# Clustered attention and a gated MLP on one core: the attention loop in four stages of three units a pair instead of six periods of two

## The chip, the cores and the metric

The kernel runs on one core of one Trainium2 chip. The metric is the device time of one execution in microseconds (us), the median of three runs. A core has a matrix engine (TensorE, PE in the profile; its weight loads are shown apart as PEld), a vector engine (VectorE, DVE), a scalar engine for functions of one input (ScalarE, ACT), a general engine (GpSimd, POOL) and SyncE (SP), which here issues transfers. Each engine works through its own queue in order; they wait for one another by semaphores. Operands lie in SBUF (128 partitions); matmuls write to PSUM, which has eight banks of 512 fp32 numbers in each partition.

## What is computed

Two blocks, one after the other, all in float32:

```python
# attention: q, k, v of (4, 8, 768, 64); 16 centroids a head
q_assign = argmax(einsum('bhsd,hcd->bhsc', q_n, c_n), axis=-1)   # q_n, k_n, c_n: normalized
k_assign = argmax(einsum('bhsd,hcd->bhsc', k_n, c_n), axis=-1)
mask = q_assign[:, :, :, None] == k_assign[:, :, None, :]
scores = where(mask, q @ k^T / sqrt(64), -1e9)
attn = exp(scores - max(scores)); attn = attn / (sum(attn) + 1e-9)
out = attn @ v
# bridge to x of (3072, 512), then the MLP, w_in (512, 2048), w_out (2048, 512)
h = x @ w_in
g = h * erf(softplus(h))
return g @ w_out
```

A query sees only the keys of its own cluster.

## The kernel before

**Pairs, halves, units.** The 32 heads are taken two at a time: 16 pairs (`p`), the two heads (`e`) in the two halves of the partitions. A pair has two halves of 384 queries, and for each half six tiles of 128 keys: 12 units (`u`), 192 in all. The order of every engine's work is that of the program text: the wrapper `InOrder` (lines 50 to 64) keeps it, and line 59 is therefore the line of nearly every row of the profile. One tells rows apart by their tiles.

**What a unit needs.** `products(u)` (line 405) writes the fp32 products of keys and queries to a PSUM tile `sc`, of which there are two (line 109). `scores(u)` (line 418) adds to the same tile a bf16 product of the masks `km` and `qm`, which brings a large negative number where clusters differ and subtracts a bound on the maximum. `curve(u)` (line 431) is ScalarE's exponential from `sc` to one of eight SBUF tiles `pr`; an `sc` tile is free for the unit after next once its curve has read it. `accumulate(u)` (line 436) sums the `pr` of a half on GpSimd. `attend(u)` (line 448) multiplies `pr` with `v` on TensorE; a half's six attends add up in one of the two PSUM banks `turned`. `divide(u)` (line 460), after a half's last attend, sums over the keys with a matmul into the other `turned` bank, takes the inverse by a logarithm and an exponential on ScalarE (`inv`), refines it in two VectorE operations (one in place in that bank, one to `den`), and a third multiplies the attended half and sends it to `x_dram`. `divide` is a generator: each `next` runs one part.

**The maxima.** The bound on a query's maximum comes from a cheaper bf16 version of the scores. `maxima_step(p, i)` (line 362), 12 a pair, writes four bf16 matmuls to the one PSUM tile `wide` (two banks, line 110), and VectorE reduces it to `nmx`, 128x768 elements. After the sixth and the twelfth step a small reduction writes `lowest`, and `turn` (line 385) turns it with three matmuls against an identity into a `turned` bank, from where ScalarE copies two rows into `qm`. The steps run ahead of the units: `step_ahead(u)` (line 702) does the step six units on.

**Clusters.** For the pair after next `transposes` (VectorE) turns q and k, `similarities` (TensorE, four matmuls of 32 columns a tile) writes to `turned[1]`, `choose` (four VectorE operations) finds the nearest centroid, `vectors` (two ScalarE casts) makes the bf16 copies `qv` and `kv`. `masks` (line 345), four a pair for the pair after, is one matmul into a `turned` bank and one ScalarE copy to `qm` or `km`.

**The loop.** `period(p, i)` (line 711), six a pair, takes two units: step, products of both, step, scores of both, curves of both, then the attends of the two units before, and after periods 0 and 3 the matmuls of `divide`. Masks stand at four places by the table `MASKS`.

**Work for the MLP on the side.** The weights come in 512 KB pieces and go through five passes each (`size_and_rest` two on ScalarE, `bounded`, `shifted` on VectorE, `sign` on ScalarE, `summed` on GpSimd); 22 of 32 conversions run in the attention part, two a pair in pairs 0 to 10. `summed` also fetches a further piece into the freed place. From pair 11 on VectorE computes sums of weight blocks (`forms`). After pair 11 two chunks of x are loaded (`load_x`), after pair 13 the forms of the first join the list. Behind attention the MLP runs block by block on TensorE, with VectorE and ScalarE behind it.

Of the kernel before, what the change touches and what calls it, by code (L numbers as in the profile page):

```python
# [22 lines left out]
NJ = S // P  # L23
# [3 lines left out]
HJ = NJ // 2  # L27
# [15 lines left out]
SH = 2 * C  # L43
NPT = NJ + 2
N_LATE = 10
LAST_X = 11
MASKS = {(0, 1): ("k", 0), (0, 2): ("k", 1), (2, 0): ("q", 0), (5, 0): ("q", 1)}
FIRST_MASKS = {(2, 0): ("k", 0), (2, 1): ("q", 0), (2, 2): ("k", 1), (5, 0): ("q", 1)}


class InOrder:
# [16 lines left out]
def kernel(  # L68
# [104 lines left out]
    def load_qk(p):  # L173
        load(p, "q", q, stage if p != 1 else None)
        load(p, "k", k, stage if p != 1 else None)
# [40 lines left out]
    N_EARLY = len(w_steps) - N_LATE  # L216

    x_of = {n: xp.tile([P, DM // P, CT], F32, name="x_own") for n in range(2)}
    places = [x_of[n][:, i : i + 2].rearrange("p k t -> p (k t)") for n in range(2) for i in (0, 2)]
    places.append(x_more.rearrange("p a k t -> p (a k t)")[:, 0 : 2 * LC])  # L220
    place_of = {n: places[n % PLACES] for n in range(N_EARLY)}
    after_of = {n: n + PLACES for n in range(N_EARLY - PLACES)}
# [5 lines left out]
        words = t.rearrange("p (n w) -> p n w", w=2)  # L228
        steps[n] = words[:, :, 1], words[:, :, 0], t.bitcast(I16)[:, 1 : 4 * LC : 4]

    def size_and_rest(n):
        w, (hi, lo, _) = w_steps[n][0], steps[n]
        ae.activation(out=w, in_=hi, func=ACT.Abs, scale=UP)
        ae.activation(out=lo.bitcast(I32), in_=lo.bitcast(U32), func=ACT.Copy, scale=2.0**-29)

    def bounded(n):
# [56 lines left out]
    def transposes(p, which="qk"):  # L293

        if p >= NPAIR:
            return
        st = pairs[p]
        for nm in which:
            st[nm + "T"] = rows[p % 3][nm]
            ve.transpose(out=st[nm + "T"], in_=st.pop(nm).rearrange("p n t -> p (n t)"))  # L300
        if "k" in which:
            st.update(lows[p % 2])
            if p > 1:
                load_qk(p + 1)

    def similarities(p):

# [37 lines left out]
    def masks(p, nm, half, bank):  # L345

        if p >= NPAIR:
            return lambda: None
        st = pairs[p]
        cols = slice(half * HW, (half + 1) * HW)  # L350
        r = slice(0, D) if nm == "q" else slice(D, P)
        won = bank[:, 0:HW]
        te.matmul(won, lhsT=pick[r, half], rhs=st["hotT"][r], start=True, stop=True)
        if nm == "q":
            return lambda: ae.activation(out=st["qm"][:, cols], in_=won, func=ACT.Relu)
        return lambda: ae.activation(
            out=st["km"][:, cols], in_=won, func=ACT.Identity, bias=nbig, scale=BIG
        )
# [3 lines left out]
    def maxima_step(p, i, sm=wide):  # L362

        st = pairs[p]
        nmx = maxima[p % 2]
        t, half = divmod(i, 2)
        for a, b, start in (("qv", "kv", True), ("qm", "km", False)):
            for e in range(2):
                r = slice(e * D, (e + 1) * D)
                te.matmul(  # L370
                    sm[:, e, 0:HW], lhsT=st[a][r, t * P : (t + 1) * P],
                    rhs=st[b][r, half * HW : (half + 1) * HW], start=start, stop=not start,
                )
        ve.tensor_reduce(
            out=nmx[:, :, t, half], in_=sm[:, :, 0:HW], axis=AX.X, op=ALU.max, negate=True
        )
        if i in (NJ - 1, 2 * NJ - 1):
            h = i // NJ
            ve.tensor_reduce(
                out=lowest[h][:, :, SH::D].rearrange("p t e -> p e t"),  # L380
                in_=nmx[:, :, h * HJ : (h + 1) * HJ], axis=AX.X, op=ALU.min,
            )
            turns.append((p, h))

    def turn(p, h):
# [19 lines left out]
    def products(u):  # L405
        p, half, j = units[u]
        if u in sc_of:
            return
        st = pairs[p]
        sc = sc_of[u] = ps_s.tile([P, 2, 512], F32, name="sc", tag="s")  # L410
        for e in range(2):
            r = slice(e * D, (e + 1) * D)
            te.matmul(
                sc[:, e, 0:HW], lhsT=st["kT"][r, j * P : (j + 1) * P],
                rhs=st["qT"][r, half * HW : (half + 1) * HW], start=True, stop=False,
            )
# [14 lines left out]
    def curve(u):  # L431

        pr = prs[u % NPT]
        ae.activation(out=pr[:, :, 0:HW], in_=sc_of.pop(u)[:, :, 0:HW], func=ACT.Exp, scale=D**-0.5)
# [264 lines left out]

    def step_ahead(u):
        p, i = divmod(u + NJ, 2 * NJ)
        if p < NPAIR:
            maxima_step(p, i)

    forms = sum((left_forms(ve, *w_in_parts(f, 2)) for f in range(0, HF, 2)), [])
    routing = [iter(())]
    part = [iter(())]

    def period(p, i):
        u = 2 * NJ * p + 2 * i
        n1, n2 = 2 * p, 2 * p + 1
        early = lambda n: 0 <= n < N_EARLY

        def mask(place):
            which = (MASKS if p else FIRST_MASKS).get((i, place))
            if which:
                return masks(p + 1, *which, turned[0 if i in (0, 5) else 1])
            return lambda: None  # L720

        if u > 0:
            for which in turns if i in (0, 3) else ():
                turn(*which)
                turns.remove(which)
            step_ahead(u)
        mask(0)()
        next(part[0], None)
        products(u)
        products(u + 1)  # L730
        mask(1)()
        if u > 0:
            step_ahead(u + 1)
        next(part[0], None)
        scores(u)
        scores(u + 1)
        later = mask(2)
        if i == 3:
            similarities(p + 2)
            routing[0] = choose(p + 2)  # L740
        curve(u)
        later()
        curve(u + 1)
        if u == 0:
            step_ahead(1)
            similarities(1)
            routing[0] = choose(1)
            next(routing[0])
            next(routing[0])
        if i == 0 and early(n1 - 1):  # L750
            shifted(n1 - 1)
        elif i == 1 and early(n1):
            size_and_rest(n1)
        elif i == 2 and early(n1):
            bounded(n1)
            sign(n1)
        elif i == 3:
            if early(n1):
                shifted(n1)
            if early(n2):  # L760
                size_and_rest(n2)
        elif i == 4 and early(n2):
            sign(n2)
        elif i == 5 and early(n2):
            bounded(n2)
        if i == 3:
            for _ in range(3):
                next(routing[0], None)
        if n1 - (i == 0) >= N_EARLY and i in (0, 2, 3, 5) and forms:
            forms.pop(0)()  # L770
        if i == 0:
            if p:
                transposes(p + 2, "q")
        elif i == 1:
            load(p + 1, "v", v, vp)
            if p == 0:
                run(routing[0])
                vectors(1, "q")
                vectors(1, "k")
        elif i == 2:  # L780
            transposes(p + 2, "k" if p else "qk")
        elif i == 4:
            vectors(p + 2, "k")
        elif i == 5:
            run(routing[0])
            vectors(p + 2, "q")
        if u > 0:
            for w in (u - 2, u - 1):
                accumulate(w)
            if i == 1 and early(n1 - 1):  # L790
                summed(n1 - 1)
            elif i == 4 and early(n1):
                summed(n1)
            for w in (u - 2, u - 1):
                attend(w)
            if i % HJ == 0:
                part[0] = divide(u - 1)
                next(part[0])
        mask(3)()


    def warm(n, bank, rhs):
# [44 lines left out]
    for i in range(NJ):  # L847
# [2 lines left out]
            masks(0, "q", 1, turned[1])()  # L850
        if i < NJ - 1:
            warm(2, turned[0], zeros)
    step_ahead(0)
    warm(2, turned[0], zeros)
    turn(0, 0)
    turns.clear()
# [1 line left out]
    fetch(PLACES - 1)  # L858
    queues[0] = queues[1] = nc.sync
    for p in range(NPAIR):  # L860
        for i in range(HJ * 2):
            period(p, i)
        if p == LAST_X:
            load_x(0)
            load_x(1)
        if p == LAST_X + 2:
            forms += right_forms(ve, *x_parts(0))
    for work in forms:
        work()
    u = len(units)  # L870
    for w in (u - 2, u - 1):
        accumulate(w)
    for w in (u - 2, u - 1):
        attend(w)
    last = divide(u - 1)
    attention.close()
# [18 lines left out]

    def weights(n):
        return [
            functools.partial(w, N_EARLY + n) for w in (size_and_rest, bounded, sign, shifted, summed)
        ]

    def all_weights(lo, hi):
# [76 lines left out]
```

## Time and profile before

| | |
|---|---|
| median of three runs | 1039.59 us (1039.57 to 1039.62) |
| the profiled execution | 1039.59 us; its span is 1037.9 us |
| granted TensorE clock | 0.999 of full |
| TensorE busy, 20 to 100 us | 74.8 of 80 |
| TensorE busy, 145 to 260 us | 113.3 of 115 |
| TensorE busy, 375 to 445 us | 68.6 of 70 |
| attention's last matmuls begin | 450.3 us |
| first matmuls of the MLP | 453.1 us |
| reductions of `wide` (`nmx`) | 189, 0.956 us each |
| exponentials (`pr`) | 192, 0.810 us each |
| sums on GpSimd (`more_out`) | 128 of 1.749 us, 32 of 1.823 us |

The span is the time from the first to the last instruction in the profile. A row of the timeline has a start, a duration, an engine, an operation, the tile written and the tiles read, and at the end in brackets the idle time before it with what ended it; equal rows that follow one another are merged (x8). Matmuls are pipelined, so a row's duration is longer than the time until the next matmul can start: distances between starts tell what a matmul costs. `64*128` stands for 64 rows and 128 columns of the matrix engine used: two such matmuls, one for each head, run side by side. `128*64` is the shape of attend, where the two heads lie beside each other in the columns, and `128*32` that of the similarities. The tile `more_out` also serves as memory for other things in the attention part (the sums, some transposed q and k, the finished x).

### The profile page before, as it was taken

The page shows a single profiled execution, that of the slowest core. Times are in us where ns is not written, and L with a number is a line of the kernel's source. Part 1 is how long each engine was busy: PE and PEld are TensorE (multiplying, and loading weights), DVE is VectorE, ACT ScalarE, POOL GpSimd, SP SyncE. Part 2 cuts the span into 40 slices and gives each one's busy share as a digit, 9 for nine tenths or more (in the row PEclk, how much of TensorE's full clock was granted, in tenths as well). Part 3 has the DMA queues.
Part 4 walks back from the last instruction along what each step waited for, and adds up shares of the span by engine and source line. Part 5 has one row for each costly group of instructions (what it writes and reads, how often), then busy time and mean ns, then how long its engine had stood idle before and what let it go on. Part 6 is the DMA issues. An engine that isn't in the chain of part 4 may idle for free.

```text
span 1037.9 us, 15280 instructions
## 1 busy us (share of the span) xinstructions
PE 1018.7 (98%) x5839; PEld 722.2 (70%) x5839; DVE 697.5 (67%) x1304; ACT 516.4 (50%) x674; POOL 345.5 (33%) x229
## 2 busy tenths in 40 slices
PE   7899999999999999999999999999999999999998
PEld 3444444444444444468888888888888888888887
DVE  7777777777777777757965765567475656564754
ACT  2777777777876666557635050514232232505050
POOL 1677777777777666755130000000000000000000
PEclk9999999999999999999999999999999999999999
DMA  9244444444344211033100010010011000000001
GB/s 221 62 103 102 103 102 100 92 91 99 81 103 100 57 38 32 16 117 102 41 1 21 21 41 1 21 61 1 1 40 41 1 21 21 1 1 21 21 1 41
DMA packets 141497, 55.55 MB, mean 54 GB/s; under 512 B 127088, under 2 KB 131184, under 8 KB 141424
## 3 DMA queue, kind: packets, MB, share of 16 engines
q1 hardware_dynamic: 138288, 54.18, 20.3%
q8 instruction: 46, 0.75, 0.3%
q10 hardware_dynamic: 3136, 0.39, 0.2%
q14 instruction: 27, 0.22, 0.1%
HBM read 41.98 MB, written 12.58 MB: 53 GB/s over the span
## 4 chain that ended last, share of the span: by engine, by line
PE 89%; DVE 8%; ACT 1%; issue 1%; SPq 1%; DMA 0%; POOL 0%; DVEq 0%; ACTq 0%; POOLq 0%
PE bank L59 42%; PE turned L59 31%; PE sc L59 10%; PE wide L59 6%; DVE nmx L59 3%; DVE den L59 2%; DVE turned L59 1%; SPq L59 1%; DMA in_q<-in_q_dram 0%; POOL more_out L59 0%; DVE more_in L59 0%; DVE sims L59 0%; ACT pr L59 0%; DVE wide L59 0%; ACT inv L59 0%
## 5 line engine op out<-in xcount | busy, mean ns | idle before, releaser
L59 POOL TENSOR_TENSOR more_out<-more_out,pr 128x768 f32<-128x768 f32 x128 | 223.8, 1749 | 78.7 <-ACT pr L59 73.7
L59 DVE TENSOR_REDUCE nmx<-wide 128x2 f32<-128x768 f32 x189 | 180.8, 956 | 102.3 <-PE wide L59 75.4
L59 ACT ACTIVATE pr<-sc 128x768 f32<-128x768 f32 x192 | 147.1, 810 | 85.4 <-PE sc L59 84.1
L59 PE MATMUL turned<-pr,in_v 128*64 128x386 f32 x768 | 145.4, 500 | 6.5 <-DVE den L59 6.5
L59 DVE TENSOR_TENSOR g<-bank,g 128x256 f32<-128x256 f32 x222 | 89.6, 421 | 56.9 <-PE bank L59 46.8
L59 PE MATMUL bank<-x_own,w_in 128*128 128x256 f32 x424 | 104.4, 379 | 0.0
L59 PE MATMUL bank<-w_out,g 128*128 128x256 f32 x448 | 103.1, 379 | 0.0
L59 PEld LDWEIGHTS turned<-pr,in_v 128*64 128x64 f32 x768 | 46.6, 136 | 80.8 <-issue 61.7
L59 PE MATMUL sc<-qT,kT 64*128 64x384 f32 x528 | 99.7, 484 | 0.0
L59 PEld LDWEIGHTS bank<-w_out,g 128*128 128x128 f32 x448 | 85.1, 190 | 11.6
L59 PEld LDWEIGHTS bank<-x_own,w_in 128*128 128x128 f32 x424 | 80.4, 190 | 12.0 <-issue 0.6
L59 ACT COPY g<-bank 128x256 f32<-128x256 f32 x28 | 10.4, 372 | 151.5 <-PE bank L59 148.4
L59 DVE TENSOR_TENSOR osb<-bank,osb 128x256 f32<-128x256 f32 x87 | 35.5, 421 | 72.8 <-ACT osb L59 25.4
L59 ACT ACT_TABLE_LOAD x48 | 61.6, 1283 | 45.7 <-DVE g L59 45.1
L59 POOL TENSOR_TENSOR more_out<-pr,pr 128x768 f32<-128x768 f32 x32 | 58.3, 1823 | 63.0 <-ACT pr L59 63.0
L59 PE MATMUL bank<-x_more,more_in 128*128 128x256 f32 x296 | 76.0, 379 | 0.0
L59 PEld LDWEIGHTS <-qv 64*128 64x128 bf16 x384 | 26.8, 93 | 69.6 <-issue 53.3
L59 PE MATMUL wide<-kv,qv 64*128 64x384 bf16 x378 | 69.8, 328 | 4.6 <-DVE nmx L59 2.7
L59 PE MATMUL wide<-km,qm 64*128 64x384 bf16 x378 | 68.8, 322 | 0.0
L59 PEld LDWEIGHTS sc<-qT,kT 64*128 64x128 f32 x528 | 56.3, 187 | 16.9 <-issue 1.8
L59 PE MATMUL bank<-more_out,g_more 128*128 128x256 f32 x272 | 64.3, 379 | 0.0
L59 DVE TENSOR_TENSOR g<-a_s,g 128x512 f32<-128x512 f32 x96 | 62.5, 689 | 1.4 <-ACT a_s L59 1.4
(158 smaller groups left out, 1705.4 us busy)
## 6 DMA issues: line engine op xcount, KB each, us to landing
x_own<-in_moe_w_in_dram SPq DMA_DIRECT2D x13, 512.0 KB, 4.1
in_v<-in_v_dram SPq DMA_DIRECT2D x32, 192.0 KB, 2.9
x_dram<-more_out SPq DMA_DIRECT2D x32, 192.0 KB, 2.1
x_own<-x_dram SPq DMA_DIRECT2D x6, 1024.0 KB, 5.0
out_dram<-osb SPq DMA_DIRECT2D x24, 256.0 KB, 2.0
in_q<-in_q_dram SPq DMA_DIRECT2D x58, 96.0 KB, 3.2
in_k<-in_k_dram SPq DMA_DIRECT2D x58, 96.0 KB, 2.6
g_more<-in_moe_w_out_dram SPq DMA_DIRECT2D x6, 512.0 KB, 3.6
```

The source lines that it names most:

```text
L59: ins = getattr(self.engine, name)(*args, **kw)
```

## The change

The loop's body is replaced. `three(p, i)`, four a pair, takes three units one after the other: step, products, scores and curve of a unit before the next unit's (the third unit's step stands between its products and scores), then three attends of the stage before. Turns stand behind the first of the three attends instead of ahead of a period. The matmuls of `divide` come after stages 0 and 2. Three masks of the next pair stand in stage 0, the fourth in stage 2. The steps run seven units ahead. Similarities, the whole of `choose` and both casts are in stage 2; the k transpose moves to stage 3 for a pair further on, the q transpose stays in stage 0 and is now what the next loads of q and k follow. The 22 conversions run three in two pairs up to pair 15, with their passes regrouped; the two loads of x follow the conversions that free their memory (pairs 13 and 15), and the order of the conversion's places in that memory is swapped. Forms start at pair 9.

```diff
-LAST_X = 11
-MASKS = {(0, 1): ("k", 0), (0, 2): ("k", 1), (2, 0): ("q", 0), (5, 0): ("q", 1)}
-FIRST_MASKS = {(2, 0): ("k", 0), (2, 1): ("q", 0), (2, 2): ("k", 1), (5, 0): ("q", 1)}
+MASKS = {(0, 0): ("k", 0), (0, 1): ("q", 0), (0, 2): ("k", 1), (2, 0): ("q", 1)}
+FIRST_MASKS = {(1, 1): ("k", 0), (1, 2): ("q", 0), (2, 0): ("k", 1), (2, 2): ("q", 1)}
...
-    places = [x_of[n][:, i : i + 2].rearrange("p k t -> p (k t)") for n in range(2) for i in (0, 2)]
+    places = [x_of[n][:, i : i + 2].rearrange("p k t -> p (k t)") for n in (1, 0) for i in (0, 2)]
...
         if "k" in which:
             st.update(lows[p % 2])
-            if p > 1:
-                load_qk(p + 1)
+        if "q" in which and p > 1:
+            load_qk(p + 1)
...
-    def step_ahead(u):
-        p, i = divmod(u + NJ, 2 * NJ)
-        if p < NPAIR:
-            maxima_step(p, i)
+    ahead = [[u + NJ + 1] for u in range(len(units) - NJ - 1)] + [[] for _ in range(NJ + 1)]
+    ahead[NJ - 1] = []
+    for u in range(NJ, 2 * NJ):
+        ahead[u] = [u + NJ]
+    ahead[2 * NJ - 1].append(3 * NJ)
+
+    def steps_ahead(u):
+        for n in ahead[u]:
+            maxima_step(*divmod(n, 2 * NJ))
...
+    def conversions(p, i):
+        a = 3 * (p // 2)
+        of = {
+            (0, 0): [(bounded, a - 1), (sign, a - 1)],
+            (0, 1): [(shifted, a - 1), (size, a)],
+            (0, 2): [(bounded, a), (rest_of, a), (sign, a)],
+            (0, 3): [(size, a + 1)],
+            (1, 0): [(shifted, a), (rest_of, a + 1)],
+            (1, 1): [(bounded, a + 1), (size, a + 2)],
+            (1, 2): [(shifted, a + 1), (rest_of, a + 2), (sign, a + 1)],
+        }.get((p % 2, i), [])
+        for f, n in of:
+            if 0 <= n < N_EARLY:
+                f(n)
+
+    def converted(p, i):
+        n = 3 * (p // 2) + {(0, 3): -1, (1, 1): 0, (1, 3): 1}.get((p % 2, i), -99)
+        if 0 <= n < N_EARLY:
+            summed(n)
+            if n == N_EARLY - 4:
+                load_x(0)
+            elif n == N_EARLY - 1:
+                load_x(1)
+
+    def three(p, i):
+        u = 2 * NJ * p + 3 * i
...
+        for k in range(3):
+            if k < 2 and u + k > 0:
+                steps_ahead(u + k)
+                for _ in range(2 if k or u == 3 else 1):
+                    next(part[0], None)
+            copy = mask(k) if k == 0 else None
+            if copy:
+                copy()
+            products(u + k)
+            if k == 2:
+                steps_ahead(u + k)
+            if k:
+                copy = mask(k)
+            scores(u + k)
+            if k == 1:
+                copy()
+            curve(u + k)
+            if k == 2:
+                copy()
+            if u + k == 0:
+                steps_ahead(u)
+        if i == 2:
+            similarities(p + 2)
+            run(choose(p + 2))
+        elif i == 3:
+            transposes(p + 3, "k")
+        elif p and i == 0:
+            transposes(p + 2, "q")
...
+        conversions(p, i)
+        if (p >= 9 and i % 2 == 0 or p >= 13) and forms:
+            forms.pop(0)()
+        if i == 2:
+            vectors(p + 2, "k")
+            vectors(p + 2, "q")
...
         if u > 0:
-            for w in (u - 2, u - 1):
+            for w in range(u - 3, u):
                 accumulate(w)
...
+            converted(p, i)
+            for w in range(u - 3, u):
                 attend(w)
-            if i % HJ == 0:
+                if w == u - 3:
+                    for which in turns:
+                        turn(*which)
+                    turns.clear()
+            if i % 2 == 0:
                 part[0] = divide(u - 1)
                 next(part[0])
...
-        for i in range(HJ * 2):
-            period(p, i)
-        if p == LAST_X:
-            load_x(0)
-            load_x(1)
-        if p == LAST_X + 2:
+        for i in range(4):
+            three(p, i)
+        if p == 13:
             forms += right_forms(ve, *x_parts(0))
...
-    for w in (u - 2, u - 1):
+    for w in range(u - 3, u):
         attend(w)
```

More of the change, by code (lines that the diff above doesn't have):

```diff
@@ L229, in fetch, with size, rest_of @@
         steps[n] = words[:, :, 1], words[:, :, 0], t.bitcast(I16)[:, 1 : 4 * LC : 4]
-    def size_and_rest(n):
-        w, (hi, lo, _) = w_steps[n][0], steps[n]
+    def size(n):
+        w, (hi, _, _) = w_steps[n][0], steps[n]
         ae.activation(out=w, in_=hi, func=ACT.Abs, scale=UP)
+    def rest_of(n):
+        lo = steps[n][1]
         ae.activation(out=lo.bitcast(I32), in_=lo.bitcast(U32), func=ACT.Copy, scale=2.0**-29)
@@ L709 @@
     part = [iter(())]
[L711 to L714, printed above, removed]
+    def conversions(p, i):
[22 more added lines that the diff above has]
+        u = 2 * NJ * p + 3 * i
         def mask(place):
@@ L718, in mask @@
             if which:
-                return masks(p + 1, *which, turned[0 if i in (0, 5) else 1])
+                return masks(p + 1, *which, turned[0 if p and i == 0 else 1])
             return lambda: None
[L722 to L738, printed above, removed]
-            similarities(p + 2)
[L740 to L745, printed above, removed]
-            similarities(1)
[L747 to L769, printed above, removed]
-            forms.pop(0)()
-        if i == 0:
-            if p:
-                transposes(p + 2, "q")
+        for k in range(3):
[19 more added lines that the diff above has]
+                steps_ahead(u)
@@ new lines, in three @@
+        if i == 2:
+            similarities(p + 2)
+            run(choose(p + 2))
[3 more added lines that the diff above has]
+            transposes(p + 2, "q")
+        elif u == 0:
+            similarities(1)
+            part[0] = choose(1)
+            next(part[0])
+            next(part[0])
+        elif u == 3:
+            transposes(2)
+        conversions(p, i)
+        if (p >= 9 and i % 2 == 0 or p >= 13) and forms:
+            forms.pop(0)()
@@ L774, in period @@
+        if i == 2:
+            vectors(p + 2, "k")
+            vectors(p + 2, "q")
+        elif u == 0:
+            vectors(1, "q")
+            vectors(1, "k")
         elif i == 1:
             load(p + 1, "v", v, vp)
[L776 to L786, printed above, removed]
@@ L787, in period @@
         if u > 0:
-            for w in (u - 2, u - 1):
+            for w in range(u - 3, u):
                 accumulate(w)
[L790 to L793, printed above, removed]
-            for w in (u - 2, u - 1):
-                attend(w)
-            if i % HJ == 0:
+            converted(p, i)
+            for w in range(u - 3, u):
+                attend(w)
+                if w == u - 3:
+                    for which in turns:
+                        turn(*which)
+                    turns.clear()
@@ L797, in period @@
+            if i % 2 == 0:
                 part[0] = divide(u - 1)
                 next(part[0])
-        mask(3)()
     def warm(n, bank, rhs):
@@ L852 @@
             warm(2, turned[0], zeros)
-    step_ahead(0)
+    maxima_step(0, NJ)
     warm(2, turned[0], zeros)
@@ L870 @@
     u = len(units)
-    for w in (u - 2, u - 1):
+    for w in range(u - 3, u):
         accumulate(w)
-    for w in (u - 2, u - 1):
+    for w in range(u - 3, u):
         attend(w)
@@ L897, in weights @@
         return [
-            functools.partial(w, N_EARLY + n) for w in (size_and_rest, bounded, sign, shifted, summed)
+            functools.partial(w, N_EARLY + n) for w in (size, rest_of, bounded, sign, shifted, summed)
         ]
```

## The prediction, with its working

> **What bounds the kernel now.** I read the page first: TensorE's share, and the chain of work that ended last.
>
> ```profile
> PE 1018.7 (98%) x5839; PEld 722.2 (70%) x5839; DVE 697.5 (67%) x1304; ACT 516.4 (50%) x674; POOL 345.5 (33%) x229
> PE 89%; DVE 8%; ACT 1%; issue 1%; SPq 1%; DMA 0%; POOL 0%; DVEq 0%; ACTq 0%; POOLq 0%
> ```
>
> TensorE is busy 98% of the span and is 89% of the chain, so what counts is what it executes, what a change of shape costs it, and when it waits. The changed code ends with attention (to about 453 us). Next, the busy times by stretch, one row per pair of heads (total, then PE, PEld, DVE, ACT, POOL, granted clock, DMA share, GB/s):
>
> ```profile
> 173.38:200.38 27.00, 26.62 (x198) 13.07 (x202) 20.09 (x31) 21.09 (x33) 19.95 (x13) 1.00 0.43 98
> 362.50:389.85 27.35, 26.65 (x200) 12.99 (x199) 21.58 (x31) 16.62 (x26) 17.97 (x11) 1.00 0.17 41
> ```
>
> A pair takes 27.0 us, at full clock; TensorE alone is full. Then the timeline of one period (two units), TensorE first and VectorE behind it (start, duration, what, count):
>
> ```profile
> 188.72 0.82 PE L59 MATMUL turned<-more_out,minus 128*64 128x384 f32 x4
> 189.47 0.34 PE L59 MATMUL wide<-kv,qv 64*128 64x384 bf16 x2
> 189.65 0.33 PE L59 MATMUL wide<-km,qm 64*128 64x384 bf16 x2
> 189.81 1.45 PE L59 MATMUL sc<-qT,kT 64*128 64x384 f32 x8
> 191.10 0.33 PE L59 MATMUL wide<-kv,qv 64*128 64x384 bf16 x2
> 191.26 0.33 PE L59 MATMUL wide<-km,qm 64*128 64x384 bf16 x2
> 191.42 0.49 PE L59 MATMUL sc<-qm,km 64*128 64x384 bf16 x4
> 192.09 1.52 PE L59 MATMUL turned<-pr,in_v 128*64 128x386 f32 x8 [0.18 <-DVE den L59]
> 193.54 0.34 PE L59 MATMUL wide<-kv,qv 64*128 64x384 bf16 x2
> ...
> 190.01 0.96 DVE L59 TENSOR_REDUCE nmx<-wide 128x2 f32<-128x768 f32 x1 [1.01 <-PE wide L59]
> 190.89 0.56 DVE L59 SCALAR_TENSOR_TENSOR turned<-turned,inv 128x384 f32<-128x384 f32 x1
> 191.48 0.56 DVE L59 SCALAR_TENSOR_TENSOR den<-turned,inv 128x384 f32<-128x384 f32 x1
> 191.95 0.95 DVE L59 TENSOR_REDUCE nmx<-wide 128x2 f32<-128x768 f32 x1
> ```
>
> Differences of starts give TensorE's prices: a maxima step 0.34, products 1.29 for two units (0.645 each), scores 0.163 each, attend 0.648 a unit. Two units of attend take 1.45 (192.09 to 193.54), not 1.30: the first pair of matmuls takes 0.05 more, leaving for the next shape 0.10. Entering costs 0.09 (0.25 from the last score's start, where nothing waits, against 0.16). So a visit to attend costs 0.24 beyond its work. In this period entry is late by 0.26 more: attend's bank is the one that `den` still reads.
>
> The key interval is between two steps. A step starts at 189.47, its reduction at 190.01 (0.54 later), for 0.96, and the next step starts at 191.10: 1.63 apart. Both write the single tile `wide`. How close may they come? The one place where a step really waited, in the prologue (TensorE, then VectorE):
>
> ```profile
> 16.99 0.34 PE L59 MATMUL wide<-kv,qv 64*128 64x384 bf16 x2
> 18.54 0.34 PE L59 MATMUL wide<-kv,qv 64*128 64x384 bf16 x2 [0.20 <-DVE nmx L59]
> ...
> 17.54 0.95 DVE L59 TENSOR_REDUCE nmx<-wide 128x2 f32<-128x768 f32 x1
> ```
>
> The step follows 0.05 after the reduction's end, 1.55 after the step before on that tile. So 0.54 + 0.96 + 0.05 = 1.55 us is the least interval, and the kernel's 1.63 just clears it.
>
> **The change, part by part.** I call the four stages of `three` 0 to 3, their units a, b, c. TensorE's order becomes step a, products a, scores a, step b, products b, scores b, products c, step c, scores c, three attends, and divide's matmuls after stages 0 and 2.
>
> *Removed.* Two visits to attend a pair: 2 × 0.24 = 0.48. The two waits for `den`: 2 × 0.26 = 0.52, since attend now starts about 4 us after divide's matmuls, and `den` is read about 3.3 us after them. The last k mask's wait for its bank in period 0, some 0.18 (a score-to-mask distance of 0.51 against 0.33).
>
> *Added: the step's wait.* From step a to step b lie 0.34 + 0.645 + 0.163 = 1.14 us, against 1.55 needed. TensorE waits 0.41 in each stage; behind it stand products b and all that follows, and nothing of it can be passed. In stages 0 and 2 it hides the mask of place 0 (0.16).
>
> *Added: the reduction of b queued behind divide.* In stages 1 and 3 `next(part[0])` puts both divide operations after reduction a: 1.41 and 2.00 (0.87 and 1.47 after reduction a's start, as at 190.01). Reduction b can start only at 2.48 instead of 2.09, ends 3.43, and step c starts 3.48 instead of 3.34: 0.14. In stage 3 ScalarE is late too. Stage 2 gives it a mask copy, three curves, two conversion passes, both casts and divide's logarithm and exponential. Counted by start-to-start distances: curve c 3.93 to 4.63, 0.56, 1.09, 0.80, 0.85 to 7.92; logarithm and exponential 1.14 to 9.06. Stage 3 starts at 7.59, so the inverse is there at 1.47 of it, the divide operations run from 1.63, and step c starts at 3.70: 0.36. Curve a of stage 3 starts at 1.45, ends 2.26, before products c (2.70) ask for its buffer.
>
> *Moved: the turns.* They now stand between two attends, with other shapes on both sides. No row shows turn followed by attend. Lower bound: as today (0.27, no more), upper: a full second visit, 0.24 more. I take the sum of seen parts, exit 0.10, turn 0.27, first pair 0.05: 0.15 more than today, as turn-to-step is its nearest row. 2 × 0.15 = 0.3 a pair.
>
> Stage by stage (us from its step a):
>
> ```
> stage              1      2      3      0
> step b           1.55   1.55   1.55   1.55
> products c       2.70   2.70   2.70   2.70
> step c           3.48   3.34   3.70   3.51
> attends begin    4.05   4.06*  4.27   4.08     (*similarities first, +0.78)
> end              6.58   7.59   6.80   6.82     sum 27.79
> ```
>
> The ends are: three attends 2.10 (2.00 before divide), turns 0.43 in stages 1 and 3, divide 0.75 after stages 0 and 2; in stage 0 one more mask (0.16). The same prices give the present 27.0. Without the added waits (4 × 0.41, 0.14, 0.36, less 0.32 of masks no longer hidden) a pair would take 25.97. So **0.8 us more a pair**.
>
> *Moved, at no cost.* Conversions: 22 as before, now 1.5 a pair instead of 2. ScalarE loses 0.5 × 2.2 us a pair, VectorE 0.5 × 0.84, GpSimd 0.5 × 1.28; none of it is on TensorE's path except the ScalarE queue of stage 2, priced above. GpSimd has 10 sums of 1.72 and 1.5 of 1.28, 19 us of 27. Loads of q and k: the eight issues (0.4 each on SP) now follow the q transposes in stage 0; k is wanted in stage 3, 14 us on, and lands in about 3. Were that cover gone, the k transpose would delay VectorE and with it step a. The two loads of x (1 MB, 5.0 us to land) go to pairs 13 and 15; the forms on the first run in pair 15, the second is used far into the MLP. The forms (0.68, beside a GpSimd sum up to 1.33) stand at the end of VectorE's stages 0 and 2 in pairs 9 to 12 and in every stage from 13. Stage 2's VectorE work ends 7.7 without a form, 8.3 to 9.0 with; the next reduction is due at 8.13. Between 0 and 0.6 a pair: I take 1.5 us in all, of 0 to 4.
>
> *Ends.* Prologue and pair 0: scores first, then two steps in a row (1.2 waited), the routing of pair 1 after; I reach the first divide at 40.5 against 40.3 now, ±3. Last pair: no steps from unit 5 on, so by the same prices its stages 1 to 3 take 6.12, 5.44 and 4.80, and three attends (1.95) end the work: 18.3 us from the end of its first divide, against 21.0 now (with a `den` wait of 0.67).
>
> *Sum.* From the first divide to that of pair 15: 14 × 27.79 + 6.80 + 6.82 = 402.7, less 1.3 for pairs 14 and 15 (no similarities, casts, masks), plus 1.5 forms = 402.9, against 391.0 now (+11.9). With +0.2 at the start, -2.7 at the end and -0.4 at the handover (ScalarE's first copy there waits for GpSimd's last sum, which ends 1.8 us after TensorE's attention, then about level), +9.0. The profiled execution spans 1037.9 and took 1039.59, 1.7 outside the span, the same as the median. Span 1046.9, time **1048.6 us**.
>
> The Trainium skill, Perfetto Trace Analysis, section Matmuls (under Optimizing Tensor Performance), asks that independent matmul groups rotate through several PSUM banks, so that one's evacuation overlaps the next's matmuls. By this rule alone `wide` is the fault of both kernels alike, the wait is in both, and the sum would be only the savings, near 1022; by the rows above, one tile costs nothing at 1.63 apart and 0.41 at 1.14.
>
> **Rivals.** (1) *The step wait does not show* and only the removed visits count: 25.97 a pair, 1.82 × 14.5 = 26 us less, 1022. For it: TensorE's order puts a mask there in stage 0, and 98% busy leaves little else to win. Against it: the prologue's 1.55, and no step in the attention of the profile follows its predecessor closer. It decides if step b starts within 1.25 us of step a. (2) *Half of it shows*, because entries, turns or ScalarE come out cheaper than priced: 27.2 a pair, about 1040. (3) *ScalarE becomes the bound of stage 3*: the signs take 1.36 to 1.40 instead of 1.09 (a start-to-start distance of 1.39 also occurs), the logarithm slips, curve a starts past 1.8, products c wait; 0.3 to 1 us a pair more, about 1058. Against it: 0.4 us of slack.
>
> **How the numbers follow.** Forecast 0.70, (1) 0.09, (2) 0.08, (3) 0.13. The forecast's own range is 1042 to 1055 (turns ±4, start ±3, forms 0 to 4); reaching into (2) and (3), 1038 to 1059, with about 0.17 left out. A measurement of this kernel tells about 0.2% (2.1 us) from no change. Faster: (1) and a little of (2), 0.10; same, the rest near 1040, 0.06; slower 0.84.
>
> **What would show it.** In the changed profile: waits of PE on `wide` for the reduction about 60 times 0.4 us; step b 1.55 after step a; step c 3.5 to 3.7 after step a in the stages after a divide; no wait for `den`; a pair near 27.8. I am wrong if pairs take under 27, or if products wait for the curve.

## The result, and the profile after

| | before | after |
|---|---|---|
| median | 1039.59 us (1039.54 to 1039.62, 5 runs) | 1065.64 us (1064.07 to 1065.72, 5 runs) |
| ratio, 95% interval | 1 | 1.0248 (1.0233 to 1.0262) |
| profiled execution, its span | 1039.59, 1037.9 us | 1064.07, 1062.0 us |
| first matmuls of `divide` | 40.30 | 43.53 |
| from there to the first ones that run in pair 15 (for the second half of pair 14) | 390.98 | 413.16 |
| from there to the MLP's first matmul | 21.78 | 20.54 |
| the MLP part | 584.8 | 584.8 |

The kernel became 2.5% slower; 1048.6 us was forecast, with a range up to 1059. The sign is right, the size too small by 17 us. The profiled execution is the fastest of the five (spans of the others are 1063.4 to 1063.7, at a granted clock of 0.998 instead of 1.0), so against its span of 1062.0 the forecast span of 1046.9 is 15.1 short: 3.0 at the start (40.5 forecast), 10.3 in the pairs (402.9), 1.5 at the end (19.05, which is 18.3 and the 0.75 of `divide`'s matmuls), and 0.3 at the handover to the MLP, whose -0.4 did not come.

The page of the changed kernel, its first part and the engines' shares of the chain of waits:

```profile
PE 1022.6 (96%) x5839; PEld 715.1 (67%) x5839; DVE 724.1 (68%) x1304; ACT 525.7 (50%) x674; POOL 344.2 (32%) x229
...
PE 79%; DVE 12%; ACT 4%; issue 2%; SPq 1%; DMA 0%; DVEq 0%; ACTq 0%
```

TensorE executes the same 5839 matmuls, but it is 79% of the chain instead of 89%, VectorE 12% instead of 8% and ScalarE 4% instead of 1%. VectorE's busy time rose by 26.6 us (697.5 to 724.1), though it has the same 1304 instructions: some of them got longer. The change gives it no new work, so this is the first thing to explain. By operation, 16.5 us of the rise are two-input operations of 128x512 elements, the shape of the forms, and 10.5 are the conversion passes `bounded` and `shifted`.

The busy times of two pairs by stretch, an early one without forms and a later one with some (total, then PE, PEld, DVE, ACT, POOL, clock, DMA share, GB/s):

```profile
198.65:226.59 27.94, 26.84 (x197) 12.50 (x196) 20.56 (x29) 20.58 (x31) 18.67 (x12) 1.00 0.35 77
282.32:310.98 28.66, 26.83 (x196) 12.55 (x195) 22.87 (x32) 20.57 (x30) 20.46 (x13) 1.00 0.39 92
```

The clock is full in both. The early pair, 27.94, is close to what the forecast's stage table gives (27.79). The later one takes 0.72 more, and the column that grew most is VectorE's, by 2.31 us; three forms fall into it, wholly or in part.

Stage 1 of the early pair shows the forecast's mechanism. TensorE first, VectorE's reductions behind it:

```profile
198.65 0.34 PE L58 MATMUL wide<-kv,qv 64*128 64x384 bf16 x2
198.82 0.33 PE L58 MATMUL wide<-km,qm 64*128 64x384 bf16 x2
198.98 0.81 PE L58 MATMUL sc<-qT,kT 64*128 64x384 f32 x4
199.63 0.33 PE L58 MATMUL sc<-qm,km 64*128 64x384 bf16 x2
200.20 0.34 PE L58 MATMUL wide<-kv,qv 64*128 64x384 bf16 x2 [0.25 <-DVE nmx L58]
...
202.13 0.34 PE L58 MATMUL wide<-kv,qv 64*128 64x384 bf16 x2
...
205.25 0.34 PE L58 MATMUL wide<-kv,qv 64*128 64x384 bf16 x2
```

```profile
199.19 0.96 DVE L58 TENSOR_REDUCE nmx<-wide 128x2 f32<-128x768 f32 x1 [1.11 <-PE wide L58]
200.06 0.56 DVE L58 SCALAR_TENSOR_TENSOR turned<-turned,inv 128x384 f32<-128x384 f32 x1
200.65 0.56 DVE L58 SCALAR_TENSOR_TENSOR den<-turned,inv 128x384 f32<-128x384 f32 x1
201.13 0.95 DVE L58 TENSOR_REDUCE nmx<-wide 128x2 f32<-128x768 f32 x1
```

Step b starts at 200.20, 1.55 after step a and 0.05 after the end of the reduction; behind the scores at 199.63 it could have come 0.16 later, at 199.79, so 0.41 is lost, as priced. Step c comes at 3.48 of the stage, which lasts 6.60. The waits ranked by what was waited for say the same:

```profile
PE wide L58 <- DVE nmx L58: 24.8, 44, 1.6
```

Before, that wait counted 2.7 us in 5 places. (The list also holds the waits that a late VectorE makes longer, up to 1.6 us, and leaves out those under 0.15, so its sum is not 44 times the 0.41.) The waits of TensorE for `den` (6.5 us in 31 places before) are gone. So far the prediction holds. Now the same place at the start of the later pair, VectorE, then GpSimd, then TensorE:

```profile
281.67 2.17 DVE L58 TENSOR_TENSOR more_in<-w_in 128x512 f32<-128x512 f32 x1
283.76 0.94 DVE L58 TENSOR_REDUCE nmx<-wide 128x2 f32<-128x768 f32 x1
```

```profile
281.54 1.75 POOL L58 TENSOR_TENSOR more_out<-more_out,pr 128x768 f32<-128x768 f32 x1
```

```profile
282.32 0.34 PE L58 MATMUL wide<-kv,qv 64*128 64x384 bf16 x2
...
284.76 0.34 PE L58 MATMUL wide<-kv,qv 64*128 64x384 bf16 x2 [1.14 <-DVE nmx L58]
```

A form, 0.68 us where it is alone, starts 0.13 after a sum on GpSimd and takes 2.17. The reduction behind it starts at 283.76 instead of 282.86 (0.54 after step a), and step b follows step a by 2.44 instead of 1.55. The stage has no slack for it.

### The profile page after: what moved, and what is told of

The parts are those of the page before. It is cut to its first block, busy times and chain, and to the rows that moved or that the text cites. A ratio compares the mean times of both kernels' runs of the same rounds, so it can differ in the third digit from the quotient of the medians.

```text
span 1062.0 us, 15287 instructions
## 1 busy us (share of the span) xinstructions
PE 1022.6 (96%) x5839; PEld 715.1 (67%) x5839; DVE 724.1 (68%) x1304; ACT 525.7 (50%) x674; POOL 344.2 (32%) x229
## 4 chain that ended last, share of the span: by engine, by line
PE 79%; DVE 12%; ACT 4%; issue 2%; SPq 1%; DMA 0%; DVEq 0%; ACTq 0%
PE bank L58 41%; PE turned L58 24%; PE sc L58 8%; DVE nmx L58 7%; PE wide L58 6%; ACT pr L58 1%; DVE more_in L58 1%; ACT inv L58 1%; ACT kv L58 1%; SPq L58 1%; DVE den L58 1%; DVE turned L58 1%; DVE w_out L58 1%; ACT qv L58 1%; DVE w_in L58 0%
## 5 line engine op out<-in xcount | busy, mean ns | idle before, releaser
L58 POOL TENSOR_TENSOR more_out<-more_out,pr 128x768 f32<-128x768 f32 x128 | 218.1, 1704 | 44.3 <-ACT pr L58 37.4
L58 ACT ACTIVATE pr<-sc 128x768 f32<-128x768 f32 x192 | 155.3, 810 | 86.9 <-PE sc L58 83.9
L58 PE MATMUL sc<-qT,kT 64*128 64x384 f32 x528 | 112.2, 484 | 0.4 <-ACT pr L58 0.4
L58 PEld LDWEIGHTS <-qv 64*128 64x128 bf16 x384 | 29.3, 93 | 115.9 <-issue 107.4
L58 PE MATMUL wide<-kv,qv 64*128 64x384 bf16 x378 | 65.7, 328 | 30.3 <-DVE nmx L58 24.8
L58 PE MATMUL sc<-qm,km 64*128 64x384 bf16 x384 | 71.8, 322 | 0.7 <-ACT qm L58 0.7
L58 PE MATMUL wide<-km,qm 64*128 64x384 bf16 x378 | 65.1, 322 | 0.0
```

Source lines behind the costliest of these rows:

```text
L58: ins = getattr(self.engine, name)(*args, **kw)
```

## The experiments

Kernels 1, 2, 3 and 5 are edits of the changed kernel, 4, 6, 7 and 8 of the kernel before. Those with one run were profiled in it; a pair is measured between the `divide` matmuls of its first half and those of the next pair.

**1. The forms moved within the stage.** They stand right behind reduction a of stages 0 and 2, when VectorE waits for step b anyway; only the forms of odd stages from pair 13 on stay at the end of a stage.

```diff
                 for _ in range(2 if k or u == 3 else 1):
                     next(part[0], None)
+                if k == 0 and p >= 9 and i % 2 == 0 and forms:
+                    forms.pop(0)()
...
-        if (p >= 9 and i % 2 == 0 or p >= 13) and forms:
+        if p >= 13 and i % 2 and forms:
             forms.pop(0)()
```

> The changed kernel with the forms of stages 0 and 2 moved from the stage's end (beside GpSimd's sums, 2.17 us each in the changed kernel's trace) to right behind reduction a (GpSimd idle there). Theory A (the excess over the forecast in pairs 9 to 13 is VectorE being late because a form takes 2.17 us beside a running GpSimd sum): forms there take 0.68, pairs 9 to 12 fall from 28.7 to 29.7 us to 27.9 to 28.1, the time falls by 5 to 8 us to about 1058. Theory B (it is the conversions, which now also run in the late pairs): the late pairs stay at 28.5 or more, time within 2 us of 1065.

Measured: 1055.75 us (span 1053.7; the kernel before 1039.51 beside it, one run each), 9.9 less than the changed kernel's median, and 8.3 less by the spans of the two profiled executions: a little more than the 5 to 8 expected. The tenth to the thirteenth pair took 27.94, 27.79, 27.95 and 27.79, like those without forms, instead of 28.82, 28.67, 29.71 and 28.69. VectorE's timeline at one form:

```profile
289.47 0.96 DVE L58 TENSOR_REDUCE nmx<-wide 128x2 f32<-128x768 f32 x1 [1.13 <-PE wide L58]
290.34 0.68 DVE L58 TENSOR_TENSOR more_in<-more_in,w_in 128x512 f32<-128x512 f32 x1
291.02 0.96 DVE L58 TENSOR_REDUCE nmx<-wide 128x2 f32<-128x768 f32 x1
```

and GpSimd's around it:

```profile
292.77 1.83 POOL L58 TENSOR_TENSOR more_out<-pr,pr 128x768 f32<-128x768 f32 x1 [2.90 <-ACT pr L58]
```

GpSimd was idle from 289.87 to 292.77; the form took 0.68, and the next reduction started at 291.02, 1.55 after the one before: nothing is late. The same forms, at the same rate, cost nothing at another place of the stage. What they cost was their place. The conversion passes are as long here as in the changed kernel, or nearly so (9.3 us over the kernel before instead of 10.5), and these pairs still take what the stage table gives: that part of VectorE's rise costs them nothing.

**2. No form in the loop.** All twenty run behind it.

```diff
         conversions(p, i)
-        if (p >= 9 and i % 2 == 0 or p >= 13) and forms:
-            forms.pop(0)()
```

> The changed kernel with no form in the loop: all 20 run behind it, so the handover to the MLP waits and only the pairs count. Theory A: every pair from 2 to 13 takes 27.8 to 28.0 us. Theory B (conversions in late pairs): pairs 9 to 13 stay at 28.5 or more. From the first to the last divide of pairs 0 to 15: A 402 to 404 us, B 411 or more (changed kernel 413.2).

Measured: 1066.33 us. From the first `divide` matmuls to those of pair 15 it took 403.85 (44.83 to 448.68), and every pair up to the thirteenth took 27.78 to 27.95, apart from the first with its 29.03 (the tenth to the thirteenth agree with those of kernel 1 within 0.01); the last pair took 19.80 to the MLP. So in the changed kernel the forms cost 413.16 - 403.85 = 9.3 us in the pairs and 20.54 - 19.80 = 0.7 at the end. The total is no better because the forms now hold up the MLP: from its first matmul (468.48) to the end of the span (1064.2) lie 595.7 us instead of 584.8. TensorE waits 9.03 of it for `x_more`, the output of the last forms; the granted clock was 0.84 between 468.5 and 500, which can account for the rest.

**3. Half a reduction.** The changed kernel with a cheaper reduction of `wide`: a price of the interval itself.

```diff
-            out=nmx[:, :, t, half], in_=sm[:, :, 0:HW], axis=AX.X, op=ALU.max, negate=True
+            out=nmx[:, :, t, half], in_=sm[:, :, 0 : HW // 2], axis=AX.X, op=ALU.max, negate=True
```

> The changed kernel with every step's reduction reading only half of its columns (half of the keys left out of the maximum), so that it takes about 0.56 us instead of 0.96. Theory A (TensorE waits for the one tile between steps a and b): step b follows step a 1.14 to 1.2 us later, a pair falls from 27.9 to about 26.8, not to the 26.0 of no waits because in stage 3 ScalarE's inverse is then late; time 1040 to 1050. Theory C (the loss lies in changes of shape or in the order on TensorE itself): pairs stay above 27.5.

Measured: 1043.61 us, and 26.60 to 26.91 for the pairs without forms after the first. A stage's first two steps on TensorE:

```profile
198.25 0.34 PE L58 MATMUL wide<-kv,qv 64*128 64x384 bf16 x2
...
199.41 0.47 PE L58 MATMUL wide<-kv,qv 64*128 64x384 bf16 x2
```

The reduction takes 0.56, and step b comes 1.16 after step a with no wait; a pair loses 1.1 us. That confirms that the reduction's length sets step b. What remains above the 25.97 of rival (1) is partly ScalarE in stage 3, which shows once the wait no longer covers it, on VectorE:

```profile
180.65 0.57 DVE L58 SCALAR_TENSOR_TENSOR turned<-turned,inv 128x384 f32<-128x384 f32 x1 [0.62 <-ACT inv L58]
```

The inverse is 0.62 late there, and step c comes 2.24 after step b where the work between them is 1.79 (0.34 + 0.645 + 0.163 + 0.645). These 0.45 are not the whole of the 0.8 by which a pair exceeds 25.97; the rest was not traced.

**4. The kernel before, with the new order in its periods of two.** Products, scores and curve of a unit come together, and the second step behind them.

```diff
         products(u)
-        products(u + 1)
+        scores(u)
+        curve(u)
         mask(1)()
...
         next(part[0], None)
-        scores(u)
+        products(u + 1)
         scores(u + 1)
...
-        curve(u)
         later()
```

> The kernel before, six periods of two units, with one part of the change alone: a unit's scores right behind its products, so that the second step follows the first after 1.14 instead of 1.63 us. Theory A: each period waits about 0.4 us (six a pair, less what masks hide and the waits for the denominator that vanish): a pair takes 28.2 to 28.8 against 27.0, time 1058 to 1068. Theory D (the loss comes from grouping by three): pairs within 0.3 us of 27.0, time under 1045.

Measured: 1063.05 us, 28.60 a pair, 1.6 more than before, and the step interval is again the least one (TensorE):

```profile
188.32 0.34 PE L59 MATMUL wide<-kv,qv 64*128 64x384 bf16 x2
...
189.87 0.34 PE L59 MATMUL wide<-kv,qv 64*128 64x384 bf16 x2
```

Once in each of the six periods instead of four stages the wait is paid. The order of products and scores is what costs; the stages of three, with fewer waits and visits to attend, give some of it back.

**5. Step b later.** On top of kernel 1, products b go ahead of step b, so that the steps lie further apart; and in pair 0 the last mask comes one unit earlier.

```diff
-FIRST_MASKS = {(1, 1): ("k", 0), (1, 2): ("q", 0), (2, 0): ("k", 1), (2, 2): ("q", 1)}
+FIRST_MASKS = {(1, 1): ("k", 0), (1, 2): ("q", 0), (2, 0): ("k", 1), (2, 1): ("q", 1)}
...
         for k in range(3):
+            if k == 1:
+                products(u + k)
...
-            products(u + k)
+            if k != 1:
+                products(u + k)
```

> The kernel of e1 with two edits. First, products b ahead of step b instead of behind it, so that steps a and b stand 1.79 us apart. Theory A (three steps share one tile, and 1.55 us must lie between any two): step b no longer waits, but step c then has to wait until 1.55 after step b, 3.34 of the stage, where it stood already; a pair of 2 to 8 stays within 0.15 of 27.87. Theory E (only the place of step b was wrong): a pair falls by 1 us or more. Second, in pair 0 the last mask of pair 1 comes a unit earlier, so that its copy on ScalarE no longer holds up the similarities: the first divide comes at 42.0 to 42.6 instead of 43.5; if that wait was not the cause, at 43.5.

Measured: 1057.97 us beside 1039.59 for the kernel before. The steady pair became 28.13 to 28.31, 0.3 more than in kernel 1, where theory A allowed 0.15. TensorE, then VectorE's reduction of step b:

```profile
177.40 0.34 PE L58 MATMUL wide<-kv,qv 64*128 64x384 bf16 x2
...
179.19 0.48 PE L58 MATMUL wide<-kv,qv 64*128 64x384 bf16 x2
...
180.89 0.34 PE L58 MATMUL wide<-kv,qv 64*128 64x384 bf16 x2
```

```profile
179.88 0.96 DVE L58 TENSOR_REDUCE nmx<-wide 128x2 f32<-128x768 f32 x1 [0.98 <-PE sc L58]
```

Step b now comes 1.79 after step a and does not wait, but step c comes 1.70 to 2.00 after step b and does, 0.05 after the end of the reduction: between b and c only one unit's scores and products are left (1.15 with the step itself), as between a and b before. The wait moved on and grew; neither order of products b frees the stage. It grew because the reduction of b comes late in every stage: here at 179.88, 0.69 after step b instead of 0.54 (the stage's mask, whose start coincides with that of products a, is the likely cause), and in stages 1 and 3 behind the two divide operations. The other half of the edit went the way expected and further: the first `divide` matmuls came at 41.54 instead of the 43.54 of kernel 1, where 42.0 to 42.6 was expected. The moved products act in that stretch too, so the mask's own share of the 2.0 us is not separated.

**6. The kernel before without its wait for `den`.** In `divide` the first refining operation writes to SBUF, so that the PSUM bank is free one operation earlier.

```diff
-            out=psum, in0=psum, scalar=S * EPS, in1=inv, op0=ALU.subtract, op1=ALU.mult
+            out=den, in0=psum, scalar=S * EPS, in1=inv, op0=ALU.subtract, op1=ALU.mult
...
-            out=den, in0=psum, scalar=2.0, in1=inv, op0=ALU.add, op1=ALU.mult
+            out=den, in0=den, scalar=2.0, in1=inv, op0=ALU.add, op1=ALU.mult
```

> The kernel before, with the first of divide's two refining operations writing to the SBUF tile den instead of its PSUM bank, so that attend's bank is free after one operation (about 1.97 us after the step) instead of two (2.56). If the price of 0.26 us for each wait on den was right, both waits of a pair vanish: a pair takes 26.5 against 27.0, time 1031 to 1033. If the bank is not what attend waits for, or an SBUF source makes the second operation slow enough to be late for the next reduction: 27.0 and 1039.5.

Measured: 1035.44 us (5 runs) beside 1039.59 (8 runs), ratio 0.996 (0.9946 to 0.9974); 26.88 a pair instead of 26.99, where 26.5 was expected; of the 4.15 us, 3.2 are in the pairs (those with forms gain most) and 0.9 behind the last of them. The waits for `den` are gone, and each was worth what the prediction took: the attends that used to wait begin 3.11 us after the first `divide` matmuls of a pair instead of 3.36 (174.76 to 177.87, and 175.44 to 178.80 before), and in the pair's second half 16.15 after them instead of 16.65. But the second operation now reads two operands from SBUF. In period 1 VectorE shows

```profile
190.53 1.11 DVE L59 SCALAR_TENSOR_TENSOR den<-den,inv 128x384 f32<-128x384 f32 x1
191.57 0.95 DVE L59 TENSOR_REDUCE nmx<-wide 128x2 f32<-128x768 f32 x1
```

beside GpSimd's

```profile
189.94 1.29 POOL L59 TENSOR_TENSOR w_in<-w_in,x_own 128x512 int32<-128x512 int32 x1
```

It took 1.11 instead of 0.56, and the next reduction and step came late: the products of the next period start, counted from the pair's `divide` matmuls, only 0.10 ahead of the kernel before. Most of a pair's gain was given back, by what made the forms dear in the changed kernel; kernel 8 tests this.

**7. Kernel 6 with the last k mask earlier.** The table `MASKS` has `(0, 0): ("k", 0)` instead of `(0, 1): ("k", 0)`.

> e6 with the first mask of period 0 moved ahead of the products (place 0 instead of 1), so that its ScalarE copy has left the bank when the second mask asks for it. If the 0.18 us there is that wait, a pair falls by 0.1 to 0.18 more than in e6: 26.3 to 26.4, time 1028.5 to 1031. If not, no more than e6.

Measured: 1051.64 us (4 runs), ratio 1.0116 (1.0101 to 1.0131); a miss. On TensorE the mask's matmul:

```profile
191.04 0.32 PE L59 MATMUL turned<-hotT,pick 64*128 64x384 bf16 x1 [1.03 <-DVE nmx L59]
```

The profile names VectorE. By the program the mask goes to the bank from which ScalarE reads the turn's two rows, and these two copies end at 190.99 (0.95 from 190.04), 0.05 before the mask starts; VectorE's reduction ends at 191.01. The bank is the likelier holder, since the mask writes to no tile of that reduction; no run separates the two. A mask half a period earlier meets the turn, and all behind it waits 1.03; a pair takes 28.08.

**8. Kernel 6 with GpSimd's conversion sum one period later.**

```diff
-            if i == 1 and early(n1 - 1):
+            if i == 2 and early(n1 - 1):
                 summed(n1 - 1)
```

> e6 with GpSimd's conversion sum of period 1 moved behind the two sums of period 2, so that no GpSimd operation runs when VectorE's second refining operation (now with two SBUF sources) starts in period 1. Theory F (in e6 that operation took 1.11 instead of 0.56 us since it started during GpSimd's sum and ended 0.41 after it, and this made the next reduction and step late): it takes 0.56 there, the 0.2 us late step of period 2 vanishes, a pair falls from 26.9 to 26.4 to 26.6, time 1029 to 1032. Theory G (an SBUF source is slow by itself): it stays at 1.1, a pair at 26.9, time 1035.

Measured: 1034.78 us (4 runs) beside 1039.58 (7 runs), ratio 0.9954 (0.9937 to 0.997): less than the kernel before, and 0.7 us less than kernel 6, which is within the interval. The `den` operation takes 0.56 again, as theory F said, and the 0.5 us of the two waits now lasts until the step at 198.27; yet the pair fell only to 26.76, short of the 26.4 to 26.6 expected. VectorE:

```profile
190.19 0.56 DVE L59 SCALAR_TENSOR_TENSOR den<-den,inv 128x384 f32<-128x384 f32 x1
...
195.41 1.08 DVE L59 TENSOR_SCALAR w_in<-w_in 128x512 f32<-128x512 f32 x1
```

The moved sum (194.91 to 196.20) now lies under the pass `bounded`, which takes 1.08 instead of 0.42; the k transpose and the reduction behind it slip, and the step at 198.27 waits 0.23.

## Why the prediction was right in sign and wrong in size

**The step's wait: right, to the hundredth.** 1.55 was the interval, 0.41 the loss. Kernel 3 took the reduction's length away and the wait went; kernel 4 put the same order into the old kernel and the wait came. Perfetto Trace Analysis of the Trainium skill, section Matmuls, asks that independent matmul groups rotate through different PSUM banks. The prediction set this rule against its rows, and the runs bear the rows out: with a single tile the order decides, no wait at 1.63 apart and 0.41 at 1.14. No run here gave `wide` a second one: the eight banks are taken by `sc` (four), `wide` and `turned` (two each).

**The stage table: right within 0.3 us a stage, and nearer in its sum because errors cancel.** From step a, stages 1, 2, 3 and 0 of one pair took 6.60, 7.45, 7.06 and 6.83, against 6.58, 7.59, 6.80 and 6.82. Stage 2 was cheaper (entering the similarities 0.27, not 0.39). Stage 3 took 6.91 in another pair: the inverse comes 0.21 to 0.37 late there, so ScalarE does weigh in, but by 0.1 to 0.3 us, not as the bound of rival (3); curve a of that stage starts at 1.59 to 1.74 and no products wait for it. The attend ahead of a turn takes 0.80 and the turn 0.27, as summed. Steady pairs average 27.87.

**The removed `den` wait and visits: right.** No wait for `den` is left, and the stage table, which counts on both, comes out. Kernel 6, which removes the wait for `den` alone, shows the two waits worth 0.50 in its trace (0.52 priced), though another wait took most of it away again in the time of a pair.

**The forms: the step that failed.** The prediction took "1.5 us in all, of 0 to 4", from 0.68 for a form and at most 1.33 beside a GpSimd sum. The runs put them at 9.3 in the pairs and 0.7 at the end (kernel 2), and at next to nothing in the gap of the stage (kernel 1, whose pairs are 1.7 above kernel 2's in all, from the forms left at the end of odd stages). In the changed kernel 14 of the 20 took 1.77 to 2.17, three 1.2 to 1.3, and only three 0.68. The 1.33 came from three rows of the trace of before, taken as a ceiling, where a form had started late in a sum (337.80, the sum at 336.75). Rows further on in the same trace, in its last pair, were passed over: 2.05 at 440.05, 1.92 and 2.17 behind it. The price of even the shorter ones was there too: the pair from 362.50, which the prediction prints, takes 27.35 instead of 27.00. In it VectorE's form ends late, and a step on TensorE waits:

```profile
365.14 1.33 DVE L59 TENSOR_TENSOR more_in<-more_in,w_in 128x512 f32<-128x512 f32 x1
```

```profile
367.39 0.34 PE L59 MATMUL wide<-kv,qv 64*128 64x384 bf16 x2 [0.26 <-DVE nmx L59]
```

The prediction called the prologue the one place where a step really waits. The trace of before has this wait behind each of the three forms (340.04, 367.39 and 394.73) and one of 1.75 at 37.41.

The change puts forms at a place where a sum has just begun, in most pairs. The term is 7.8 of the 10.3 us that the pairs are over, and half of what the end is over. With this term at 10, span and time would be forecast some 8.5 us higher, at 1057.1: half of the 17 us that were missing.

The Trainium skill states a rule that would have given a higher ceiling. SBUF — State Buffer, section Who interferes with whom, says that a VectorE instruction with two SBUF inputs contends with a GpSimd instruction that reads SBUF, and that the later one blocks until the other is done. By that the worst form is a whole sum and a form, 1.75 + 0.68 = 2.43 (an estimate from the rows above and the page's rule); the longest measured is 2.17, for forms that start 0.13 into a sum.

**The start: mis-sized.** 43.53 against 40.5 ± 3. In kernel 5, with the mask of pair 0 moved from the place `(2, 2)`, 2.0 of the 3.0 went away, of which the wait below can be 1.35 at most; the products moved in the same run. The mask's copy stands behind a curve on ScalarE, and the similarities, which write to the same bank, wait for it, on TensorE's timeline:

```profile
40.76 0.85 PE L58 MATMUL turned<-more_out,ccT 128*32 128x384 f32 x8 [1.35 <-ACT qm L58]
```

The remaining 1.0 was not settled.

**Two steps in a row: not seen.** Unit 11 issues two steps (the list `ahead` gives it one more), and the first pair shows 29.04 instead of 27.87. On TensorE:

```profile
47.77 0.34 PE L58 MATMUL wide<-kv,qv 64*128 64x384 bf16 x2
...
49.32 0.34 PE L58 MATMUL wide<-kv,qv 64*128 64x384 bf16 x2 [1.05 <-DVE nmx L58]
```

The prediction counted 1.2 for such a double step in the prologue and overlooked this second one. With 14 pairs at 0.08 over the table (1.1), that accounts for the pairs but for 0.2: 7.8 + 1.2 + 1.1 = 10.1 of 10.3.

**The end.** 20.54 against 19.05: 0.7 are forms; 0.8 stay open.

**The rivals.** (1) falls by the 1.55 in every stage, (2) by the steady pairs of 27.87, where it needed 27.2. Rival (3) gave 1058, nearer to the result than the forecast, but by a mechanism that the trace does not show: its nearness is luck.

## What to carry over

An operation's price depends on what runs beside it: before moving work to a "free" end of a stage, find in the trace the longest, not the usual, row of that operation, look for a wait behind it, and ask what the other engine does at the new place. When one tile is written and read in turn, the least interval (write, read, signal) is a budget: an order that puts less other work between two writes pays the difference each time, and side work belongs into the gap that this wait leaves on the reading engine. A wait that is removed by moving an operand, as in kernel 6, should be followed one step further, to who meets whom next.

## What the hardware showed that was not expected

Some VectorE operations with operands in SBUF and the GpSimd sums take turns, by these rows. A form of 0.68 us that started inside a GpSimd sum ended about 0.55 after the sum's end, wherever it had started (with at least 0.2 of the sum left): 283.84 against 283.29 in the changed kernel, 339.12 against 338.57 in the kernel before. The `den` operation of kernel 6 ended 0.41 after. The pass `bounded` took 1.08 for 0.42. The other way round, a form at 331.90 in the kernel before took its 0.68, and the sum that started 0.10 later took 2.13 instead of 1.72. Reductions that read PSUM (0.96) and the `den` operation with one operand in PSUM (0.56) show no such lengthening, and nor does a transpose from SBUF to SBUF (0.97 at 57.33 in the changed kernel, inside a sum that runs until 58.41). That VectorE is held for the whole of the sum is a reading that fits all these rows; no run tried it by itself.
